# State-major order of the sread tokens, batch 1's sums later, and a rearranged start of batch 0, in an attention and feed-forward kernel

## The chip, the cores and the metric

The kernel runs on one core of a Trainium2 chip. The metric is device time in microseconds (us) of one execution, lower is better.

Engine names: TensorE (PE in the profile, PEld for its weight loads), VectorE (DVE), ScalarE (ACT), GpSimd (POOL), SyncE (SP; SPq is its queue of DMA issues). PSUM is the memory into which the matmuls here write. The "granted clock" is the share of TensorE's full rate that the profile's clock records show; time for which there is no record counts as 1.00.

## The reference

Eight batches of eight heads. `x` holds 512 tokens of 64 values per head, `state` 32. Each attends to the other, and all 544 rows of a batch then go through one feed-forward layer.

```python
scores = scale * x @ state.T ;  a  = softmax(scores)  ; xread = a  @ state   # 512 rows a batch
scores2 = scale * state @ x.T;  a2 = softmax(scores2) ; sread = a2 @ x       # 32 rows a batch
rows = concatenate([xread, sread], axis=2)         # 544 rows a batch, 8 batches
h = rows @ w_in ;  out = (h * sigmoid(h)) @ w_out  # 4352 x 512, float32
```

## The kernel before

For batch `b`, "G1" is the first product of the feed-forward layer (with `w_in` folded into the state as `W1`), "G2" the second. `aT` holds the normalised attention weights of a batch, transposed (the other operand of G1), `stT` the transposed state, and `es` sums of the exponentials over tokens, by which sread is divided. The 32 sread rows of all 8 batches are gathered in `xmT` and done at the very end as 256 tokens, in two tiles of 128 (`tt` 0 and 1). Row `544*b + 512 + n` of the output is state `n` of batch `b`. The parts that matter:

```python
xmT = pers.tile([128, 2, 4, 128], BF16)          # token = 32 * (b % 4) + n
out_sread = out.rearrange("(bb s) m -> bb s m", s=544)
...
# start of batch 0
nc.scalar.activation(warm[:], warm[:], func=EXP, bias=0.0)        # loads the exp table (1.28 us)
nc.sync.dma_start(st0_f[:], state[0].rearrange("h n d -> n h d"))
for hg in range(2):                                               # then x, 512 KB each
    nc.sync.dma_start(x_f[:, ds(4 * hg, 4), :, :], ...)
...
cast_x(0, nc.vector, h0=0, nh=4)
pe_transpose_x(0, 0, 2, ...)       # TensorE; VectorE and ScalarE copy the halves out of PSUM
cast_x(0, nc.vector, h0=4, nh=4)
...
scores(0, 0); exps(0, 0)
pe_transpose_x(0, 1, 2, ...)
scores(0, 1); exps(0, 1)
...
def token_sums(b):                 # VectorE: es, sums of exp over the 4 tokens of a partition
    ...
def sread(b):                      # TensorE: ones x es, then x_nat x exp_nat, into ps
    ...
    nc.vector.reciprocal(rb[:], ps[:, 1, :, :, :])
    for g in range(2):
        for u in range(2):
            nc.vector.tensor_tensor(
                xmT[rows, b // 4, k2, ds(32 * (b % 4), 32)],
                ps[rows, 0, k2, u ^ g, :], rb[rows, k2, u ^ g, :], op=MULT)
...
# between batch 0 and batch 1
for ft in range(NFT):
    ...
    if ft == 4:
        token_sums(1)
    if ft == 13:
        sread(1)
    ...
    G2(0, 3, ft)
...
# steady state: batch b runs, batch n = b + 1 is prepared
    if at == (1, 0):  norm(n, hg), ...          # at = (tile, step)
    if at == (1, 8):  token_sums(n)
    if at == (2, 8):  w1_chunks(n, (0, 1), both) # VectorE and ScalarE copy W1 out of PSUM
    if at == (3, 10): sread(n)
...
# the end: store of tile 0, then tile 1 in two halves of 256 columns
nc.sync.dma_start(out_sread[ds(4 * tt, 4), ds(512, 32), :], o[:])
nc.sync.dma_start(out_sread[ds(4 * tt, 4), ds(512, 32), cols], o[:])
```

In the traces VectorE starts its instructions in the order of the program: after the change, the token sums of batch 2 (62.09 us) stand before the copies of W1 (64.92 us), as in the code.

The softmax here doesn't subtract the row's maximum and nothing guards it: scores larger than these inputs give would overflow.

## Time and profile before

| | before |
|---|---|
| time, median of the first 3 runs | 229.88 us (229.19 to 230.03) |
| span of the profiled run | 228.3 us |
| TensorE busy | 213.5 us (94%) |
| first G1 of batch 0 | 13.26 us |
| first G1 of batch 1 | 46.35 us |
| first G1 of batch 2 | 65.59 us |
| start of the last matmul | 220.94 us |
| last DMA issue; it has landed | 221.71; 227.36 us |

From the page: busy time and share of each engine, then the chain of work that ended last, by engine.

```profile
span 228.3 us, 3733 instructions
...
PE 213.5 (94%) x1462; PEld 102.4 (45%) x1488; DVE 103.2 (45%) x186; ACT 142.5 (62%) x241; POOL 45.8 (20%) x64
...
PE 88%; DVE 6%; issue 1%; ACT 1%; POOL 0%; POOLq 0%
```

By stage (the view of windows; columns: the stretch, its length, busy us and instructions of TensorE, its weight loads, VectorE, ScalarE, GpSimd, then TensorE's granted clock, the share of DMA engines that were busy, GB/s):

```profile
0.00:14.56 14.56, 11.38 (x66) 5.40 (x68) 8.17 (x22) 5.90 (x10) 9.41 (x18) 1.00 1.01 189
...
57.00:197.00 140.00, 138.42 (x948) 63.76 (x963) 68.03 (x115) 100.26 (x163) 28.42 (x36) 1.00 0.40 106
...
213.00:229.00 16.00, 8.22 (x55) 5.10 (x53) 1.54 (x3) 0.98 (x2) 0.00 (x0) 0.90 0.16 49
```

From 57 to 197 us TensorE is busy 138.4 of 140 us: nothing but less TensorE work helps there. The last row is different: 8.2 us of TensorE work in the 15.35 us that are left of the span. The same view by microseconds at the end:

```profile
220.00:221.00 1.00, 1.00 (x12) 0.84 (x9) 0.00 (x0) 0.00 (x0) 0.00 (x0) 1.00 0.28 14
221.00:222.00 1.00, 0.22 (x2) 0.00 (x0) 0.42 (x1) 0.00 (x0) 0.00 (x0) 1.00 0.20 49
...
223.00:224.00 1.00, 0.00 (x0) 0.00 (x0) 0.00 (x0) 0.00 (x0) 0.00 (x0) 1.00 0.27 101
224.00:225.00 1.00, 0.00 (x0) 0.00 (x0) 0.00 (x0) 0.00 (x0) 0.00 (x0) 1.00 0.27 95
225.00:226.00 1.00, 0.00 (x0) 0.00 (x0) 0.00 (x0) 0.00 (x0) 0.00 (x0) 0.84 0.27 96
226.00:227.00 1.00, 0.00 (x0) 0.00 (x0) 0.00 (x0) 0.00 (x0) 0.00 (x0) 0.50 0.19 66
```

TensorE's work ends at 221.2 us and VectorE's last copy at 221.7 us. After that the core waits more than 5 us for its own stores, while its 16 DMA engines show a mean share of only 0.27.

TensorE's waits (who waited for whom, us in total, times, longest):

```profile
PE ps_sr L307 <- DVE es L299: 1.2, 1, 1.2
PE ps_st L217 <- DVE st_b L124: 0.8, 1, 0.8
...
PE ps_sr L307 <- DVE es L300: 0.5, 1, 0.5
```

And what VectorE and TensorE do around those two waits for `es` (start, length, engine, line, operation; in brackets the idle time just before it and what ended it):

```profile
42.40 1.98 DVE L296 TENSOR_REDUCE es_f<-exp_nat 128x128 f32<-128x512 bf16 x2
...
44.81 0.71 DVE L300 TENSOR_TENSOR es<-es_f,es 128x256 bf16<-128x256 f32 x1
...
44.83 0.28 PE L307 MATMUL ps_sr<-es,ones 128*128 128x256 bf16 x1 [1.21 <-DVE es L299]
...
45.44 0.41 DVE L124 COPY aT<-ps_at 128x512 bf16<-128x512 bf16 x1
...
46.35 0.59 PE L376 MATMUL h_664<-aT,W_400 128*128 128x512 bf16 x2
```

Batch 1's first G1 (46.35 us) needs `aT`, which VectorE copies only at 45.44 us, after the token sums.

### The profile page before, as it was taken

What the parts mean: (1) busy time and instruction counts of PE and PEld (TensorE: products, weight loads), DVE (VectorE), ACT (ScalarE), POOL (GpSimd) and SP (SyncE); (2) the same over time, 40 slices, a digit from 0 to 9 for tenths busy, and PEclk for the clock granted to TensorE, in tenths of its full rate; (3) what the DMA queues carried; (4) which work ended last, traced back from release to release, by engine and by line L of the source; (5) the groups of instructions that cost most, each with busy time, mean ns of one, the idle gap of its engine ahead of it and who ended that gap; (6) DMA issues with size and microseconds to landing.
All of it is one profiled execution on the core that took longest, in us unless ns stands there. A gap on an engine that the chain in (4) does not pass through costs nothing.

```text
span 228.3 us, 3733 instructions
## 1 busy us (share of the span) xinstructions
PE 213.5 (94%) x1462; PEld 102.4 (45%) x1488; DVE 103.2 (45%) x186; ACT 142.5 (62%) x241; POOL 45.8 (20%) x64
## 2 busy tenths in 40 slices
PE   7799899799999999999999999999999999999970
PEld 2534335344435443544354534444444444566550
DVE  5554946960765075516552565247434634100110
ACT  2555558679865985598558856885679477444110
POOL 8380001710450045003600260025001200000000
PEclk9999999999999999999999999999999999999997
DMA  6999974585169115911591159113611311111111
GB/s 191 184 196 196 204 226 140 184 199 126 51 128 275 56 48 130 284 46 50 112 296 51 49 121 283 61 46 92 141 47 46 95 46 46 46 49 41 51 24 68
DMA packets 33933, 26.97 MB, mean 118 GB/s; under 512 B 22012, under 2 KB 27900, under 8 KB 33916
## 3 DMA queue, kind: packets, MB, share of 16 engines
q1 hardware_dynamic: 27244, 15.21, 25.6%
q0 software_dynamic: 6672, 11.54, 22.6%
q8 instruction: 11, 0.18, 0.3%
q14 instruction: 6, 0.05, 0.1%
HBM read 17.30 MB, written 8.91 MB: 115 GB/s over the span
## 4 chain that ended last, share of the span: by engine, by line
PE 88%; DVE 6%; issue 1%; ACT 1%; POOL 0%; POOLq 0%
PE o L405 46%; PE ps_sc L244 2%; PE ps_sr L317 2%; PE o_half L427 2%; PE ps_xt L185 1%; PE ps_busy L130 1%; PE o_a L405 1%; DVE rs L266 1%; DVE es_f L296 1%; PE ps_sr L307 1%; DVE rb L326 1%; DVE W_214 L124 1%; ACT exp_nat L256 1%; ACT xT_143 L122 1%; DVE x_nat_141 L101 0%
## 5 line engine op out<-in xcount | busy, mean ns | idle before, releaser
L405 PE MATMUL o<-w_out_sb,g 128*128 128x512 bf16 x489 | 132.1, 380 | 0.5
L405 PEld LDWEIGHTS <-g 128*128 128x128 bf16 x528 | 50.0, 98 | 58.6 <-issue 7.1
L124 DVE COPY o_sb<-o 128x512 f32<-128x512 f32 x17 | 11.8, 692 | 64.4 <-PE o L405 64.1
L269 POOL TENSOR_TENSOR an<-exp_nat,rc 128x512 bf16<-128x512 bf16 (+1 forms) x16 | 15.9, 1009 | 111.2 <-DVE rc L267 111.0
L326 DVE RECIPROCAL rb<-ps_sr 128x256 f32<-128x256 f32 x8 | 14.1, 1758 | 16.6 <-PE ps_sr L317 16.6
L122 ACT ACTIVATE o_sb<-o 128x512 f32<-128x512 f32 x15 | 8.9, 596 | 13.5 <-PE o L405 5.3
L296 DVE TENSOR_REDUCE es_f<-exp_nat 128x128 f32<-128x512 bf16 x16 | 15.3, 1000 | 0.0
L266 DVE TENSOR_REDUCE rs<-exp_nat 128x16 f32<-128x512 bf16 x16 | 10.6, 660 | 2.2 <-ACT exp_nat L256 1.5
L96 POOL DMA_DIRECT2D x_f<-in_x_dram x7 | 6.5, 924 | 20.6 <-DVE x_nat_486 L101 19.1
L256 ACT ACTIVATE exp_nat<-ps_sc 128x512 bf16<-128x512 f32 x16 | 8.8, 595 | 1.1 <-PE ps_sc L244 1.0
L386 PEld LDWEIGHTS <-w_in_sb 128*128 128x128 bf16 x64 | 6.3, 98 | 3.9
L256 ACT ACT_TABLE_LOAD x6 | 7.7, 1283 | 0.1
L553 ACT ACT_TABLE_LOAD x6 | 7.7, 1283 | 0.1
L330 DVE TENSOR_TENSOR xmT<-ps_sr,rb 64x64 bf16<-64x64 f32 x32 | 7.1, 222 | 0.6
L350 PEld LDWEIGHTS <-stT 64*32 64x32 bf16 x264 | 2.8, 89 | 9.1 <-issue 8.5
L130 PE MATMUL ps_busy<-busy 128*128 128x512 bf16 x11 | 5.4, 627 | 1.4 <-DVE busy L144 1.2
L405 PE MATMUL o_a<-w_out_sb,g 128*128 128x512 bf16 x15 | 5.8, 396 | 0.1
L376 PEld LDWEIGHTS <-W_214 128*128 128x128 bf16 x32 | 3.2, 106 | 5.1 <-DVE W_214 L124 1.5
L300 DVE TENSOR_TENSOR es<-es_f,es 128x256 bf16<-128x256 f32 x8 | 5.1, 638 | 0.3
L376 PEld LDWEIGHTS <-W_400 128*128 128x128 bf16 x32 | 3.1, 98 | 3.9 <-issue 0.3
L307 PE MATMUL ps_sr<-es,ones 128*128 128x256 bf16 x16 | 3.2, 273 | 1.7 <-DVE es L299 1.2
L376 PEld LDWEIGHTS <-W_1420 128*128 128x128 bf16 x32 | 3.1, 98 | 3.6 <-issue 0.2
(518 smaller groups left out, 351.1 us busy)
## 6 DMA issues: line engine op xcount, KB each, us to landing
out_dram<-o_sb SPq DMA_DIRECT2D x33, 256.0 KB, 2.4
x_f<-in_x_dram POOLq DMA_DIRECT2D x7, 1024.0 KB, 7.0
w_in_sb<-in_moe_w_in_dram POOLq DMA_DIRECT2D x3, 512.0 KB, 11.5
w_out_sb<-in_moe_w_out_dram POOLq DMA_DIRECT2D x3, 512.0 KB, 14.1
x_f<-in_x_dram SPq DMA_DIRECT2D x2, 512.0 KB, 4.4
st_f<-in_state_dram SPq DMA_DIRECT2D x8, 64.0 KB, 11.3
w_in_sb<-in_moe_w_in_dram POOLq DMA_DIRECT2D x2, 256.0 KB, 7.6
w_out_sb<-in_moe_w_out_dram POOLq DMA_DIRECT2D x2, 256.0 KB, 8.2
```

What stands on the lines that cost most here:

```text
L122: nc.scalar.activation(dst, src, func=COPY, bias=0.0)
L124: eng.tensor_copy(dst, src)
L130: nc.tensor.matmul(ps[:], busy[:, 0:128], busy[:], start=True, stop=True, skip_group_check=True)
L256: nc.scalar.activation(e[:], sc_ps[hg][:], func=EXP, bias=0.0, scale=SCALE)
L266: nc.vector.tensor_reduce(rs[:], e[:], axis=AX, op=ADD)
L269: eng.tensor_tensor(a[:, ds(c, n)], e[:, ds(c, n)], rc[:, ds(c, n)].to_broadcast([128, n, 4, NS]), op=MULT,)
L296: nc.vector.tensor_reduce(f[:, hg], exp_nat[b, hg].rearrange("p c s n -> p s n c"), axis=AX, op=ADD)
L326: nc.vector.reciprocal(rb[:], ps[:, 1, :, :, :])
L330: nc.vector.tensor_tensor(xmT[rows, b // 4, k2, ds(32 * (b % 4), 32)], ps[rows, 0, k2, u ^ g, :], rb[rows, k2, u ^ g, :], op=MULT,)
L376: nc.tensor.matmul(ps[:], W1[b][:, hg, ds(128 * ft, 128)], aT[b][:, hg, :, :], start=(hg == 0), stop=(hg == 1), skip_group_check=True,)
L405: nc.tensor.matmul(outs[tt][:], gt[b * NFT + ft][:, ds(128 * tt, 128)], w_out_sb[:, ft, :], start=(ft == 0), stop=(ft == NFT - 1), skip_gr ...
L553: nc.scalar.activation(warm[:], warm[:], func=SILU, bias=0.0)
```

## The change

Four things at once. (1) The tokens of the sread tiles go in state-major order, `4 * n + b`, so that the outermost dimension of the stores in memory is 32 states and no longer 4 batches. (2) Batch 1's token sums and sread leave the gap between batches 0 and 1. (3) State 0 is loaded from ScalarE's queue, so that SyncE can issue `x` sooner. (4) Each cast of `x` in batch 0 is split over VectorE and ScalarE, and all its transposes come before the first scores.

```diff
-    xmT = pers.tile([128, 2, 4, 128], BF16)
+    xmT = pers.tile([128, 2, 4, NS, 4], BF16)
-    out_sread = out.rearrange("(bb s) m -> bb s m", s=544)
+    out_sread = out.rearrange("(bb s) m -> s bb m", s=544)
...
+    nc.scalar.dma_start(st0_f[:], state[0].rearrange("h n d -> n h d"))
     nc.scalar.activation(warm[:], warm[:], func=EXP, bias=0.0)
-    nc.sync.dma_start(st0_f[:], state[0].rearrange("h n d -> n h d"))
...
-    cast_x(0, nc.vector, h0=0, nh=4)
-    pe_transpose_x(0, 0, 2, ...)
-    cast_x(0, nc.vector, h0=4, nh=4)
+    for hg, pool, tag in ((0, psO, "o"), (1, psH, "h1")):
+        cast_x(0, nc.vector, 0, 2, 4 * hg, 4)
+        cast_x(0, nc.scalar, 2, 2, 4 * hg, 4)
+        pe_transpose_x(0, hg, 2, ...)
...
-                    xmT[rows, b // 4, k2, ds(32 * (b % 4), 32)],
+                    xmT[rows, b // 4, k2, :, b % 4],
...
-                    xmT[:, :, kt, :],
+                    xmT[:, :, kt].rearrange("p t n b -> p t (n b)"),
...
-            nc.sync.dma_start(out_sread[ds(4 * tt, 4), ds(512, 32), :], o[:])
+            nc.sync.dma_start(out_sread[ds(512, 32), ds(4 * tt, 4), :], o[:])
...                                                  # the half stores likewise
-    pe_transpose_x(0, 1, 2, ...)                    # from between the scores of batch 0
...
-        if ft == 4:
-            token_sums(1)
-        if ft == 13:
-            sread(1)
...
                     upto(NFT * b + min(lead + ft, NFT))
+                    if b == 1 and ft == 2:
+                        token_sums(1)
+                if b == 1 and at == (1, 4):
+                    sread(1)
```

More of the change, by code (lines that the diff above doesn't have):

```diff
@@ L100, in cast_x @@
             x_nat[b] = xpool.tile([128, 4, H, D], BF16, tag="x_nat", name=f"x_nat{b}")
-        eng.tensor_copy(
+        copy(
+            eng,
             x_nat[b][:, ds(c0, nc_), ds(h0, nh), :],
@@ L190, in pe_transpose_x @@
             copy(engs[u], xT[b][:, ds(m * u, m), ds(2 * hg, 2), :], ps[:])
-    cast_x(0, nc.vector, h0=0, nh=4)
-    pe_transpose_x(0, 0, 2, lambda sh, dt, nm: psO.tile(sh, dt, tag="o", name=nm))
-    cast_x(0, nc.vector, h0=4, nh=4)
+    for hg, pool, tag in ((0, psO, "o"), (1, psH, "h1")):
+        cast_x(0, nc.vector, 0, 2, 4 * hg, 4)
+        cast_x(0, nc.scalar, 2, 2, 4 * hg, 4)
+        pe_transpose_x(0, hg, 2, lambda sh, dt, nm: pool.tile(sh, dt, tag=tag, name=nm))
     nc.vector.memset(st_f[:, :, 0:1, 0:1], 0.0)
@@ L436, in last_half @@
         copy(nc.vector, o[:], ps[:, 0 : DM // 2])
-        nc.sync.dma_start(out_sread[ds(4 * tt, 4), ds(512, 32), cols], o[:])
+        nc.sync.dma_start(out_sread[ds(512, 32), ds(4 * tt, 4), cols], o[:])
     both = (nc.vector, nc.scalar)
@@ L449 @@
     exps(0, 0)
-    pe_transpose_x(0, 1, 2, lambda sh, dt, nm: psH.tile(sh, dt, tag="h1", name=nm))
     scores(0, 1)
```

## The prediction

> **What bounds it now.** TensorE: in the page it is busy 94% of a 228.3 us span and holds 88% of the chain that ended last; from 57 to 197 us (windows view) it is busy 138.4 of 140 us. The change touches three stretches outside that.
>
> 1. Tail. The last copy ends near 221.7 us, the span at 228.3. One-microsecond windows show a DMA share of 0.20 to 0.28 from 220 to 226 us, some 96 GB/s: 512 KB drains through about 4 of 16 engines. A normal 256 KB store lands 2.05 us after issue; the last 128 KB here 5.7 us after (221.71 to 227.4). The store's outer dimension in memory is 4 batches. [...]
>
> 2. Between batch 0 and 1. The waits view: TensorE waits 1.2 us for es (cast) and 0.5 us for es (subtract), 43.6 to 45.6 us; VectorE's token sums also delay the copy of aT (45.44 us).
>
> 3. Head. First G1 matmuls at 13.3 to 14 us, behind cast, transpose, scores, exp, norm.
>
> **What the change does.**
>
> Tail: with 32 states outermost, 16 engines share each store; the last should land 1.95 us after issue instead of 5.7. Saved: 3.7 us, all on the chain. The token order inside xmT should cost nothing: the matmul still reads one contiguous row.
>
> Middle: token sums (3.0 us of VectorE) leave the gap; aT is copied at about 43.5 us, so batch 1's first G1 comes at about 44.05 instead of 46.35 us. The sread matmuls (0.68 us) return later: net 1.6 us. But VectorE gets 2.7 us (reciprocal 1.76, four multiplies 0.93) between batch 2's norm and its token sums, ahead of its W1 copies. Before, VectorE is busy almost unbroken from 59.2 to 65.7 us, and batch 2's first G1 starts at 65.59, soon after the W1 copy of 64.39 to 65.07. That copy now ends near 67.6 (old times), TensorE wants it at 66.3: a new stall of about 1.3 us. Net gain of the middle: 0.3 us (0 to 1.4).
>
> Head: x is issued 0.47 us sooner, but VectorE can't cast before its stT copies end at 5.01 us. Half casts take 0.53 and 0.34 us on VectorE, about 0.6 on ScalarE (by its 512-column copies). ScalarE then carries cast, copy, cast, copy, exp, exp: the first exp ends near 9.8 us (8.93 before), the second near 10.4 (10.87). VectorE's sums and GpSimd's multiplies then run back to back and end near 12.9 us (12.80). Gain: 0 (−0.5 to +0.4).
>
> Sum: 229.88 − 3.7 − 0.3 − 0 = 225.9; I put it at 225.8 us, 1.8% under: the middle can gain more than lose. Range 224.9 to 226.7; chances 0.30 faster by over 2%, 0.69 within, 0.01 slower.
>
> **What would show it.** Tail: DMA share near 1 in short bursts, span end 3 us after the last copy. Middle: no wait of TensorE for es near 44 us; a new wait of 1.3 us for VectorE's copy of W1 at batch 2's first G1. Head: exp of group 0 later, of group 1 earlier, first G1 within 0.5 us of 13.3.
>
> **What would make it wrong.** VectorE reaching the W1 copy sooner (no stall: 224.5); stores scattered over 4 batches writing slower than in row order; ScalarE's chain in the head shorter or longer than counted.

The tail's term stands on numbers of the trace of the kernel before. The three sread stores, with 4 batches outermost, show a share of 0.27 of the 16 engines from 223 to 226 us (0.27 × 16 = 4.3), and each one's semaphore is raised by one early landing and then 4. The normal 256 KB store before them (128 rows of 2 KB, issued at 215.03 us) landed 2.05 us after issue, and its semaphore was raised 16 times. That 16 engines would share a store with 32 states outermost was the expectation, which no trace had shown yet; the 1.95 us for the last 128 KB is an estimate, a little under the 2.05 us of twice the size. Measured were 16 landings and 2.06 us, and a share of 0.94 in a burst ("The result", experiments 1, 5 and 6).

## The result, and the profile after

The changed kernel took 226.03 us in the median of 4 runs (225.01 to 226.66); the kernel before, in the same rounds and earlier, 229.64 us (229.19 to 230.03). The ratio is 0.9837 (95% interval 0.9801 to 0.9874), clear of noise, as the interval excludes 1. A ratio here and below is the mean time of one kernel's runs over that of the other's of the same rounds, so it is not quite the ratio of the medians that are quoted. The forecast was 225.8 us.

The profiled runs, stretch by stretch (each from one trace, differences worked out from the starts). In both, TensorE reaches full rate late, at 17.4 to 17.5 us, so that they may be compared; "The clock" below shows that this was not sure to happen.

| stretch | before | after | difference |
|---|---|---|---|
| start to first G1 of batch 0 | 13.26 | 13.46 | +0.20 |
| to first G1 of batch 1 | 33.09 | 30.91 | −2.18 |
| to first G1 of batch 2 | 19.24 | 21.30 | +2.06 |
| to start of the last matmul | 155.35 | 155.37 | +0.02 |
| to the end of the span | 7.41 | 3.81 | −3.60 |
| span | 228.35 | 224.85 | −3.50 |

So up to the last matmul the changed kernel has gained nothing (220.94 against 221.04 us); the whole gain comes after it. The end, in the same view as above:

```profile
220.00:221.00 1.00, 1.00 (x11) 0.89 (x10) 0.03 (x1) 0.00 (x0) 0.00 (x0) 1.00 0.50 186
221.00:222.00 1.00, 0.31 (x3) 0.03 (x1) 0.42 (x1) 0.00 (x0) 0.00 (x0) 1.00 0.39 131
222.00:223.00 1.00, 0.00 (x0) 0.00 (x0) 0.00 (x0) 0.00 (x0) 0.00 (x0) 1.00 0.00 1
223.00:224.00 1.00, 0.00 (x0) 0.00 (x0) 0.00 (x0) 0.00 (x0) 0.00 (x0) 1.00 0.38 130
224.00:225.00 1.00, 0.00 (x0) 0.00 (x0) 0.00 (x0) 0.00 (x0) 0.00 (x0) 1.00 0.00 0
```

Now each store is a short burst (from about 219.6, 221.2 and 223.0 us on), and the engines are idle between them, so that a window of 1 us shows the mean of both. The repeat of the changed kernel (experiment 4) has a half microsecond that a burst fills, at a share of 0.94 and 356 GB/s:

```profile
219.50:220.00 0.50, 0.50 (x7) 0.45 (x5) 0.25 (x1) 0.00 (x0) 0.00 (x0) 1.00 0.94 356
```

SyncE issues the last store at 221.80 us and it has landed at 223.86 us, 2.06 us later; before the change it was 5.65 us.

TensorE's waits after the change: both waits for `es` are gone, a wait for W1 is new, and the wait for the cast of the state (`st_b`, in batch 0) is longer, 1.1 us against 0.8. The third line is new too: state 0 now lands later (experiment 9).

```profile
PE h L378 <- DVE W L125: 1.1, 1, 1.1
PE ps_st L219 <- DVE st_b L125: 1.1, 1, 1.1
...
PE ps_st L163 <- DVE st_n L125: 0.5, 1, 0.5
```

The gap between the batches, and then the new wait. `aT` is copied at 43.81 us, G1 starts at 44.37 us; but at 64 us VectorE still has the token sums of batch 2 to do, and TensorE stands idle for 1.10 us until it has copied W1:

```profile
43.81 0.42 DVE L125 COPY aT<-ps_at 128x512 bf16<-128x512 bf16 x1 [0.96 <-PE ps_at L288]
...
44.37 0.81 PE L378 MATMUL h<-aT,W 128*128 128x512 bf16 x3
```

```profile
59.09 1.69 DVE L328 RECIPROCAL rb<-ps_sr 128x256 f32<-128x256 f32 x1
...
60.82 1.24 DVE L332 TENSOR_TENSOR xmT<-ps_sr,rb 64x64 bf16<-64x64 f32 x4
...
62.09 2.01 DVE L298 TENSOR_REDUCE es_f<-exp_nat 128x128 f32<-128x512 bf16 x2
...
64.47 0.43 DVE L302 TENSOR_TENSOR es<-es_f,es 128x256 bf16<-128x256 f32 x1
64.92 1.29 DVE L125 CAST W<-ps_w 128x512 bf16<-128x512 f32 x2
...
65.67 0.61 PE L378 MATMUL h<-aT,W 128*128 128x512 bf16 x2 [1.10 <-DVE W L125]
```

The first two of these lines, the reciprocal and the four multiplies of batch 1's sread, are what was put in front. The multiplies that write `xmT` have become slower (minimum, median, maximum in ns), before and then after:

```profile
L330 DVE TENSOR_TENSOR xmT<-ps_sr,rb x32: 216/222/228, 24.2 to 189.9; 64x64 bf16<-64x64 f32 x32
```

```profile
L332 DVE TENSOR_TENSOR xmT<-ps_sr,rb x32: 291/300/310, 24.3 to 190.2; 64x64 bf16<-64x64 f32 x32
```

### The profile page after: what moved, and what is told of

It is laid out like the page before. It is cut to its first block, busy times and chain, and to the rows that moved or that the text cites. A ratio compares the mean times of both kernels' runs of the same rounds, so it can differ in the third digit from the quotient of the medians. Undisturbed runs are those within 1.5% of the kernel's fastest.

```text
span 224.8 us, 3735 instructions
## 1 busy us (share of the span) xinstructions
PE 214.2 (95%) x1462; PEld 102.1 (45%) x1488; DVE 104.4 (46%) x186; ACT 143.5 (64%) x243; POOL 45.4 (20%) x64
## 4 chain that ended last, share of the span: by engine, by line
PE 86%; DVE 6%; ACT 3%; DMA 1%; issue 1%; POOL 0%; DVEq 0%; ACTq 0%
PE o L407 45%; PE h L378 25%; PE ps_w L352 4%; PE h L388 3%; PE o_half L429 2%; PE ps_sc L246 2%; DVE rb L328 2%; PE ps_sr L319 1%; DMA st_f<-in_state_dram 1%; PE o_a L407 1%; PE ps_xt L186 1%; DVE xmT L332 1%; DVE W L125 1%; DVE es_f L298 1%; ACT exp_nat L258 1%
## 5 line engine op out<-in xcount | busy, mean ns | idle before, releaser
L399 ACT ACTIVATE g<-h 128x512 bf16<-128x512 f32 (+1 forms) x144 | 82.2, 573 | 45.0 <-PE h L378 30.7
L378 PE MATMUL h<-aT,W 128*128 128x512 bf16 x256 | 76.5, 383 | 1.7 <-DVE W L125 1.1
L125 DVE COPY o_sb<-o 128x512 f32<-128x512 f32 x17 | 11.8, 692 | 62.7 <-PE o L407 62.5
L378 PEld LDWEIGHTS <-W 128*128 128x128 bf16 x256 | 25.0, 99 | 32.1 <-DVE W L125 3.1
L125 DVE CAST W<-ps_w 128x512 bf16<-128x512 f32 (+1 forms) x31 | 20.0, 676 | 18.5 <-PE ps_w L352 18.5
L123 ACT ACTIVATE W<-ps_w 128x512 bf16<-128x512 f32 (+1 forms) x35 | 18.7, 575 | 9.4 <-PE ps_w L352 9.3
L125 POOL CAST x_nat<-x_f 128x512 bf16<-128x512 f32 x24 | 14.7, 646 | 0.0
L352 PE MATMUL ps_w<-w_in_sb,stT 64*32 64x512 bf16 (+1 forms) x264 | 11.5, 383 | 0.0
L332 DVE TENSOR_TENSOR xmT<-ps_sr,rb 64x64 bf16<-64x64 f32 x32 | 9.6, 300 | 0.6
L388 PE MATMUL h<-xmT,w_in_sb 128*128 128x256 bf16 x64 | 9.6, 273 | 0.0
## 6 DMA issues: line engine op xcount, KB each, us to landing
w_out_sb<-in_moe_w_out_dram POOLq DMA_DIRECT2D x3, 512.0 KB, 13.3
```

What stands on the lines that cost most here:

```text
L123: nc.scalar.activation(dst, src, func=COPY, bias=0.0)
L125: eng.tensor_copy(dst, src)
L332: nc.vector.tensor_tensor(xmT[rows, b // 4, k2, :, b % 4], ps[rows, 0, k2, u ^ g, :], rb[rows, k2, u ^ g, :], op=MULT,)
L352: nc.tensor.matmul(pss[f, hg][ds(32 * s, 32), 0:n], stT[ds(r, 64), b, h // 2, s % 2, :], w_in_sb[ds(r, 64), h // 2, ds(f, n)], start=True, ...
L378: nc.tensor.matmul(ps[:], W1[b][:, hg, ds(128 * ft, 128)], aT[b][:, hg, :, :], start=(hg == 0), stop=(hg == 1), skip_group_check=True,)
L388: nc.tensor.matmul(ps[:, 0:256], w_in_sb[:, kt, ds(128 * ft, 128)], xmT[:, :, kt].rearrange("p t n b -> p t (n b)"), start=(kt == 0), stop ...
```

## The experiments

Each edit is against the kernel named. Times are medians with their range; the kernel before was timed in the same rounds on the same chip (its medians were 229.2 to 229.9 us).

### 1. The stores alone: `tail`

The kernel before with part (1) of the change and nothing else.

```diff
-    out_sread = out.rearrange("(bb s) m -> bb s m", s=544)
+    out_sread = out.rearrange("(bb s) m -> s bb m", s=544)
...      # with it xmT's tile, its write and read, and the three stores, as in the change
```

> The kernel before with the state-major order alone (token order of xmT and the three stores of the sread rows). Theory (the gain is all in the last stores, because they use 16 engines instead of 4): 3.5 us less than the kernel before, ratio 0.984 to 0.986, span end about 2.5 us after the last copy instead of 6.6; the xmT writes 0.30 us each instead of 0.22. Rival (the middle and the head carry some of the gain): less than 2.5 us saved.

Measured: 226.08 us (225.65 to 227.32, 6 runs) against 229.19, ratio 0.9855 (0.9812 to 0.9899). From the start of the last matmul to the end of the span 3.80 us, against 7.41 in the kernel before. This one part is as fast as the whole change, whose repeat on the same chip is at 0.9858 (experiment 4). The span ends 3.06 us after the last copy, where 2.5 were expected. The theory stands: the gain is in the stores.

### 2. The middle alone: `mid`

The kernel before with part (2) alone.

```diff
-        if ft == 4:
-            token_sums(1)
-        if ft == 13:
-            sread(1)
...      # batch 1: token_sums(1) at tile 0, step 2; sread(1) at tile 1, step 4
```

> The kernel before with batch 1's token sums and sread moved later, alone. Theory (2.3 us won at batch 1's first G1, given back as 0.68 us of sread matmuls and a new wait of TensorE for VectorE's copy of W1 at batch 2's first G1): within 0.6 us of the kernel before, the first G1 of batch 1 at 44.05 us instead of 46.35, the new wait 1.1 to 1.4 us. Rival (the gap was worth 1.6 us and the stall seen in the changed kernel comes of its other parts): 1.3 us or more saved.

Measured: 229.68 us (228.44 to 230.55, 6 runs) against 229.19, ratio 0.9997 (0.9952 to 1.0043). First G1 of batch 1 at 44.03 us. The new wait for W1 is there, 0.9 us (1.1 to 1.4 were expected), with 0.4 us more for `aT`; from the first G1 of batch 1 to that of batch 2 it is 21.15 us instead of 19.24. In the traces the 1.9 us are given back in full; the timed runs alone would leave room for a gain or loss of 1 us.

### 3. The head alone: `head`

The kernel before with parts (3) and (4).

```diff
-    nc.sync.dma_start(st0_f[:], ...)             # and on ScalarE's queue instead
-    cast_x(0, nc.vector, h0=0, nh=4)             # and the loop over both halves instead
-    pe_transpose_x(0, 1, 2, ...)                 # from between the scores
```

> The kernel before with the head alone: state of batch 0 on ScalarE's queue, casts on two engines, transposes in one row. Theory: no gain, 0 to 0.4 us slower: the state lands near 3.7 us instead of 2.76, so VectorE's stT copies end 0.5 us later and its first cast with them, and ScalarE's chain does the rest. Rival (the head won something and other parts hid it): 0.3 us or more faster.

Measured: 229.89 us (228.79 to 231.09, 6 runs) against 229.19, ratio 1.0009 (0.9959 to 1.0059). No gain. First G1 of batch 0 at 13.46 us. The interval is too wide to tell 0 from a loss of 0.4 us; the traces say more, below. ScalarE's chain in batch 0, first in the kernel before and then with the new head (these lines are from the trace of the changed kernel, whose head is the same; `head` itself shows them at most 0.07 us later): there are two more copies of 0.6 us in it (the casts, at 5.02 and 7.63 us), so that the first exp starts 1.1 us later and both end at 10.63 us, where the second ended at 10.87.

```profile
8.33 0.60 ACT L256 ACTIVATE exp_nat<-ps_sc 128x512 bf16<-128x512 f32 x1 [0.48 <-PE ps_sc L244]
...
10.27 0.60 ACT L256 ACTIVATE exp_nat<-ps_sc 128x512 bf16<-128x512 f32 x1 [0.49 <-PE ps_sc L244]
```

```profile
5.02 0.63 ACT L123 ACTIVATE x_nat<-x_f 128x512 bf16<-128x512 f32 x1 [2.31 <-DMA x_f<-in_x_dram]
...
7.63 0.62 ACT L123 ACTIVATE x_nat<-x_f 128x512 bf16<-128x512 f32 x1
...
8.95 0.60 ACT L123 ACTIVATE xT<-ps_xt 128x512 bf16<-128x512 bf16 x1 [0.70 <-PE ps_xt L186]
9.44 1.19 ACT L258 ACTIVATE exp_nat<-ps_sc 128x512 bf16<-128x512 f32 x2
```

### 4. The changed kernel again: `again`

No edit.

> The changed kernel once more, because its four runs fell into two pairs (225.0 and 225.4; 226.6 twice). If the spread is noise of the runs, 225.0 to 226.7 again with a mean near 225.9; if one pair was a rare state, nearly all runs in one of them.

Measured: 226.48 us (225.34 to 227.27, 6 runs), ratio 0.9858 (0.9815 to 0.9901). The spread is that of the first four runs, a little wider (to 227.27), and every kernel that was timed several times shows one of 0.7 us or more; where it comes from is asked under "the clock" below.

### 5 and 6. Batch-major order, other cuts of the store: `store_2b` and `store_1b`

The kernel before, token order as it was, each store cut by batches: `m = 2` gives two DMAs of two batches, `m = 1` four of one batch.

```diff
-        nc.sync.dma_start(out_sread[ds(4 * tt, 4), ds(512, 32), cols], o[:])
+        for i in range(0, 4, m):
+            nc.sync.dma_start(
+                out_sread[ds(4 * tt + i, m), ds(512, 32), cols], o[ds(32 * i, 32 * m), :])
```

> The kernel before, batch-major order kept, each sread store cut into two of 2 batches. Theory [...]: 2 engines instead of 4, about 24 GB/s each, so 512 KB drain in 10 to 11 us instead of 5.4: about 5 us slower, DMA share near 0.13 in the tail. Rival (the 4-batch stores were slow because of their row addresses or their extra issue time): no such doubling.

> The kernel before, batch-major order kept, each sread store cut into four of 1 batch. Theory: outermost size is then 32, so all 16 engines: 2.0 to 3.6 us faster than before; what is missing to 3.6 us is the issue of three more stores (0.33 us each at least, and the last one lands about 2 us after its own issue). VectorE's xmT writes stay at 0.22 us. Rival (state-major addresses themselves are what writes fast): at most 1 us faster.

Measured: `store_2b` 234.92 us (one look), 5.6 us more than the 229.32 of the kernel before; `store_1b` 227.21 us (226.65 to 227.84, 4 runs), ratio 0.9896 (0.9862 to 0.9929), 2.1 us less. The end of `store_2b` in two-microsecond windows (the columns as above):

```profile
220.00:222.00 2.00, 0.16 (x2) 0.00 (x0) 0.42 (x1) 0.00 (x0) 0.00 (x0) 1.00 0.13 44
...
224.00:226.00 2.00, 0.00 (x0) 0.00 (x0) 0.00 (x0) 0.00 (x0) 0.00 (x0) 0.50 0.13 38
...
228.00:230.00 2.00, 0.00 (x0) 0.00 (x0) 0.00 (x0) 0.00 (x0) 0.00 (x0) 0.50 0.14 48
```

The share is halved, 0.13 to 0.14 where it was 0.27, and so is the rate: 38 to 50 GB/s where it was some 96. Of the core's 16 engines these shares make about 2 (0.13 × 16 = 2.1) and about 4 (0.27 × 16 = 4.3), with 2 and 4 batches outermost in memory; the bursts of the state-major stores, with 32 states outermost, make 15 (0.94 × 16, in `again`). The rates agree: a packet of 2 KB took 84 ns in the tail of the kernel before (the median from 221 us on), which is 24.4 GB/s, so that 2 at a time make 49 GB/s and 4 make 98. The packed traces show the same order in another count: leaving out one early update in the first two, the semaphore of the very last store is raised by 4 landings in the kernel before (226.55 to 227.36 us), by 2 in `store_2b` (230.79 and 231.66 us), and by 16 in `store_1b` and in the changed kernel (223.68 to 223.86 us there). The same bytes to the same addresses from the same partitions are slower with two batches in a DMA than with four, and faster with one, an order that no account by row addresses gives. What other sizes than these would do, no run here shows; so the general rule that the expectation of `store_2b` gave is cut. `store_1b` wins less than the state-major store because SyncE issues its DMAs one after the other: the last is issued at 223.54 us instead of 221.80, and lands at 225.09 us. From the start of its last matmul (221.05 us) to the end of the span it is 4.95 us, against 7.41 in the kernel before and 3.81 in the changed one.

### 7. The stall taken out: `later`

The changed kernel, with batch 2's token sums moved behind its first W1 copies on VectorE.

```diff
-                    if at == (1, 8):
+                    if at == ((2, 10) if b == 1 else (1, 8)):
                         token_sums(n)
```

> The changed kernel with batch 2's token sums moved from tile 1, step 8 to tile 2, step 10, behind its first W1 copies on VectorE. Theory (VectorE's queue makes TensorE wait for W1): the wait of 0.9 to 1.1 us at batch 2's first G1 is gone, first G1 of batch 2 about 20.2 us after that of batch 1 instead of 21.3; 0.9 to 1.1 us faster than the changed kernel, ratio to the kernel before 0.980 to 0.982. Rival (another wait lies right behind it: aT's transpose, a PSUM bank): less than 0.4 us gained.

Measured: 225.12 us (224.64 to 225.72, 6 runs) against 229.32, ratio 0.9805 (0.9777 to 0.9833). TensorE has no wait for W1 left; first G1 of batch 2 comes 20.06 us after that of batch 1, instead of 21.30. VectorE copies W1 first (62.60 us), TensorE's G1 follows at 64.77 us without a wait, while VectorE is still at its sums:

```profile
62.60 1.29 DVE L125 CAST W<-ps_w 128x512 bf16<-128x512 f32 x2 [0.18 <-PE ps_w L352]
...
63.92 1.98 DVE L298 TENSOR_REDUCE es_f<-exp_nat 128x128 f32<-128x512 bf16 x2
...
64.77 0.59 PE L378 MATMUL h<-aT,W 128*128 128x512 bf16 x2
...
66.26 0.43 DVE L302 TENSOR_TENSOR es<-es_f,es 128x256 bf16<-128x256 f32 x1
```

So the gain of the middle was real, and of the 2.06 us that were given back 1.24 were due to VectorE's queue order. The other 0.82, the 0.68 us of sread matmuls among them, stay. This is read from the traces: the ratios point the same way, but their intervals overlap (0.9777 to 0.9833 here, 0.9815 to 0.9901 for `again`).

### 8. Which side of `xmT` pays for the order: `contig`

The changed kernel, with `xmT` written as before and read with steps by the matmul.

```diff
-    xmT = pers.tile([128, 2, 4, NS, 4], BF16)
+    xmT = pers.tile([128, 2, 4, 4, NS], BF16)
-                    xmT[rows, b // 4, k2, :, b % 4],
+                    xmT[rows, b // 4, k2, b % 4, :],
-                    xmT[:, :, kt].rearrange("p t n b -> p t (n b)"),
+                    xmT[:, :, kt].rearrange("p t b n -> p t n b"),
```

> The changed kernel with xmT written in batch order (contiguous) and read in state order by the matmul (32 elements apart). Theory (the 0.30 us of the writes comes of their 8-byte steps): writes back at 0.22 us, and the first wait for the state cast 0.8 us again instead of 1.1. Open: whether TensorE reads the strided columns as fast; if it does, its 64 matmuls stay at 273 ns and the last stage at its length; if not, they are longer.

Measured: 245.84 us (one look). The writes are back at 222 ns and the wait for the state's cast at 0.8 us, as expected, but the 64 matmuls that read `xmT` take more than twice as long:

```profile
L388 PE MATMUL h<-xmT,w_in_sb x64: 587/607/608, 196.0 to 231.9; 128*128 128x256 bf16 x64
```

In the changed kernel the same line has a median of 273 ns. The last matmul starts at 240.25 us instead of 221.04, 19 us later. Reading bfloat16 at steps of 64 bytes is what costs (607 ns against 273); writing it at steps of 8 bytes costs 0.08 us an instruction (300 ns against 222, or 35%). Why either is slower, no run here shows.

### 9. The head without the moved state load: `casts`

The kernel before with part (4) alone; the state is still issued first, by SyncE.

```diff
-    cast_x(0, nc.vector, h0=0, nh=4)             # and the loop over both halves instead
-    pe_transpose_x(0, 1, 2, ...)                 # from between the scores
     nc.sync.dma_start(st0_f[:], ...)             # stays
```

> The kernel before with casts on two engines and transposes in one row, but the state load still first on SyncE's queue. Theory (in the head, moving the state load is what costs, as it then travels beside x and lands at 3.72 us instead of 2.76): the state lands near 2.8 us again, VectorE's stT copies end near 5.0 us and its first half cast starts there instead of at 5.58; first G1 0.3 to 0.5 us sooner than with the whole head in the same clock state (13.46 us when TensorE is at half rate until 17 us), total within 1 us of the kernel before. Rival (ScalarE's chain of cast, copy, cast, copy sets the pace whatever the state does): first G1 at 13.3 to 13.5 us in that clock state.

Measured: 229.52 us (229.23 to 229.93, 4 runs) against 229.89, ratio 0.999 (0.9955 to 1.0025). The state landed at 2.59 us and VectorE's `stT` copies ended at 5.01 us, as the theory has it. But in this run `x` landed only at 5.56 us, so the casts began at 5.58 us all the same, and the first G1 was at 13.46 us to the hundredth as in the whole head. The forecast of 0.3 to 0.5 us fell. What can be said is that the chain from the casts on sets the 13.46 us; the price of the state load by itself stays open.

What the state load does can still be read from all traces. With the old order of issue (eight traces) the state landed at 2.59 to 2.76 us and the first half of `x` at 4.68 to 4.98 us in six of them, at 5.02 and 5.56 in two. With the state on ScalarE's queue (all six traces) the state landed at 3.72 to 4.23 us and `x` at 4.99 to 5.52 us, though its issue is 0.47 us sooner. Issuing them side by side made the state later and `x` no sooner.

### 10. The fast middle and stores with the old head: `later_oldhead`

Parts (1) and (2) and the edit of experiment 7, on the kernel before:

```diff
-                    if at == (1, 8):
+                    if at == ((2, 10) if b == 1 else (1, 8)):
                         token_sums(n)           # parts (3) and (4) left out
```

> The kernel before with the state-major stores, batch 1's sums later and batch 2's token sums behind its W1 copies, but the old head. Theory (the new head is worth nothing, the stores 3.5 us, the middle without its stall 1.3 us): as fast as the same with the new head (225.1 us there), within 0.4 us; ratio to the kernel before near 0.980. Rival (the new head helps once the stall is gone): over 0.5 us slower than that.

Measured: 224.60 us (224.42 to 225.13, 5 runs) against 229.89, ratio 0.9776 (0.9742 to 0.9811), the lowest ratio, with the change's head left out. The intervals of this run and of `later` (0.9805) overlap. Those of this run and of `tail` (0.9855, 0.9812 to 0.9899), which has the stores alone, do not, if only just: the mended middle is worth something in the timed runs too.

### 11 and 12. More warm-up matmuls: `fill` and `oldhead_fill`

`fill` is `later` with three more full-size warm-up matmuls in the head; `oldhead_fill` is `later_oldhead` with one. "Warm-up" is only the name here for the matmuls of `keep_busy`, whose result is not used; whether more of them bring the clock up sooner is what was to be tested.

```diff
# fill
-    keep_busy(6, psH, "h1")
+    keep_busy(7, psH, "h1")
-    keep_busy(3, psH, "h1")
+    keep_busy(4, psH, "h1")
         pe_transpose_x(0, hg, 2, ...)
+        if hg == 0:
+            keep_busy(1, psA, "a3")
# oldhead_fill
-    keep_busy(3, psH, "h1")
+    keep_busy(4, psH, "h1")
```

> The changed kernel with batch 2's token sums later and three more warm-up matmuls in the head (one before the state's transposes, one after, one between the two rows of transposes of x). Theory (the 1 to 2 us of spread of every kernel comes of TensorE's clock in the head: at half rate until 17 us in some runs, at full rate from 4.5 us in others): [...]mean 0.3 to 0.9 us below the 225.1 us without them, first G1 near 12 us. Rival (the fillers only take TensorE's time, the clock does what it did): same mean within 0.3 us or slower, spread as before.

> The fastest form so far (old head, state-major stores, batch 1's sums later, batch 2's token sums behind its W1 copies) with one more warm-up matmul, in the 0.6 us in which TensorE otherwise waits for the first cast of x (5.58 to 6.17 us). Theory [...]: 224.0 to 224.6 us, highest run under 225.0. Rival (one matmul does not change the lottery of the clock): 224.4 to 225.2 as without it, ratio near 0.978.

Measured: `fill` 224.48 us (224.32 to 225.24, 5 runs), ratio 0.9779 (0.9747 to 0.9811), on the same chip and rounds as `later_oldhead` and equal to it. Its median is 0.64 us under that of `later` (225.12), as forecast, but that was another chip, and the intervals of the two ratios overlap. First G1 of its profiled run at 13.31 us, not near 12, though its clock was full from 7.12 us. `oldhead_fill` 224.24 us (223.87 to 226.16, 6 runs), ratio 0.9799 (0.9765 to 0.9832): five runs at or under 224.74, one at 226.16, where the forecast had none above 225.0. Both are inconclusive: they are among the fastest kernels, and neither shows that the added matmuls are the reason.

### The clock

Why does every kernel spread by 0.7 us and more? In the profiled runs TensorE starts at half rate (a warm-up matmul of 512 columns every 0.43 us) and reaches full rate (0.22 us) at very different times. Two traces of kernels whose heads are the same, first that of the kernel before, then that of `store_1b`; each shows three warm-up matmuls and then four matmuls of batch 0's first two G1:

```profile
4.12 1.46 PE L130 MATMUL ps_busy<-busy 128*128 128x512 bf16 x3
...
13.26 1.31 PE L376 MATMUL h_248<-aT,W_214 128*128 128x512 bf16 x2
...
14.36 1.06 PE L376 MATMUL h_253<-aT,W_214 128*128 128x512 bf16 x2
```

```profile
4.10 0.82 PE L130 MATMUL ps_busy<-busy 128*128 128x512 bf16 x3
...
11.81 0.38 PE L376 MATMUL h<-aT,W 128*128 128x512 bf16 x1
...
12.49 0.81 PE L376 MATMUL h<-aT,W 128*128 128x512 bf16 x3 [0.30 <-DVE aT L124]
```

In the kernel before the rate doubles near 17 us; in `store_1b` at 4.0 us; in `tail` and `mid` it doubles at 4.2 to 4.3 us, falls back at 7.6 to 7.7 us and stays down for 10.24 us (the exact times here and in the table are those of the clock records in the packed traces). In `store_1b`, `tail` and `mid` the rise comes 2.75 to 3.05 us after the first matmul (1.23 us). The clock records of five traces show drops to half rate, of 3.41, 6.83 (`later`) or 10.24 us (`tail`, `mid`). What sets the time of the rise and the length of the drops is not shown. The page alone can mislead here: it gives a granted clock of 1.00 over the first 14.56 us of the kernel before, whose matmuls run at half rate there, because the clock records of that trace start only at 17.47 us; the spacing of the matmuls is what to trust.

The record has one more sign that the clock makes the spread. Each timed run has a mean granted clock. Of the ten runs of the changed kernel (`after` and `again`), the five at 1.000 took 226.36 to 226.66 us, the three at 0.999 took 225.01 to 225.44 (the other two, at 0.992 and 0.985, took 225.80 and 227.27); in `later` the three at 1.000 took 225.11 to 225.12 us, the two at 0.984 took 225.71 and 225.72. In `oldhead_fill`, though, three runs at 0.992 took 224.09, 224.39 and 226.16. How often each case occurs, and that it makes up the whole spread, no run here shows.

First G1 of batch 0, sorted by it:

| clock in the head | old head | new head |
|---|---|---|
| half rate past the first G1 (full from 16.6 to 17.5 us) | 13.26 (before) | 13.46 (after, `head`, `casts`), 13.45 (`again`) |
| half rate until 11.68 us | none | 13.88 (`contig`) |
| full early, dropped at 7.6 to 7.7 us | 12.84 (`tail`), 12.85 (`mid`) | none |
| full from 7.1 us or sooner, up to 11.8 us at least | 11.81 (`store_1b`), 12.00 (`later_oldhead`), 12.14 (`store_2b`), 12.17 (`oldhead_fill`) | 12.84 (`later`), 13.31 (`fill`) |

At half rate the new head is 0.2 us slower (`contig` is not comparable: its clock rose before the first G1, and `x` landed late, at 5.52 us). At full rate there are two traces of it, `fill`, which has more matmuls in its head than any other, and `later`, whose clock fell back at 11.88 us. `later` is some 0.7 us or more behind: GpSimd's last multiply, ahead of that first G1, ends at 12.38 us, against 11.52 (`store_1b`) and 11.71 us (`later_oldhead`). A faster TensorE shortens only its own share of the chain, and the new head has put two casts of 0.62 us onto ScalarE's share. That this is the whole reason was only argued.

## Why the prediction was right, point by point

- **Total.** 225.8 us was forecast, 226.03 measured (226.48 in the repeat). Right, and within 2% as the likeliest case. That it fits to 0.2 us is partly luck: the four runs fall into two pairs (225.01 and 225.44, 226.62 and 226.66), and the median lies between them. In the two traces the difference is 3.50 us, where the parts of the forecast add up to 4.0.
- **Tail.** Forecast 3.7 us, measured 3.60 us in the traces; the last store lands 2.06 us after issue (1.95 forecast), the span ends 3.1 us after the last copy (3). Experiments 1, 5 and 6 show that the number of engines is the cause (2, 4 and 16 landings at 48, 96 and, in a burst, 356 GB/s). A part of the old tail was a slow start: from 220 to 221 us the DMA engines were as busy as later (a share of 0.28) but moved 14 GB/s; in the same microsecond `mid` shows 18 GB/s at 0.30, `head` and `casts` 8 GB/s at 0.18. Why is open; the traces with state-major stores have no such microsecond.
- **Middle.** Forecast: first G1 of batch 1 2.3 us sooner, 0.68 us of sread matmuls back, a new stall of 1.3 us. Measured: 2.18 us less from G1 to G1 in the first stretch, 2.06 us more in the second, of which 1.10 us are the stall and 0.68 the matmuls; 0.28 us are not accounted for. Experiment 2 gives the net 0 by itself (in its trace; its timed runs do so within 1 us), and experiment 7 removes the stall and keeps the gain.
- **Head.** Forecast 0, and first G1 within 0.5 us of 13.3: it came at 13.46. The reasoning had two errors. It expected the cast to begin at 5.01 us, when `stT` was done; but the state, now beside `x`, landed 1 us later, and the copies ended at 5.55. And it took the clock of the one trace it had for the clock of all runs; at full rate the new head seems to lose more.
- **The step that was wrong:** "The token order inside xmT should cost nothing". The read by the matmul costs nothing (273 ns before and after), but the write does: 300 ns instead of 222, 1.24 instead of 0.93 us for a batch, which TensorE sees twice. In batch 0 it waits 0.3 us more for the state's cast that stands behind them (`tail` 1.1 us, `contig` 0.8). And batch 1's multiplies stand in front of batch 2's W1 copy: from batch 1's first G1 to batch 2's it is 20.98 us in `contig`, which writes in the old order, against 21.30 in the changed kernel. So they took a part of the middle's gain as well. It is the small term of a sum of 3.6 us.

## What to carry to other kernels

Look at the outermost dimension in memory of the last stores of a kernel: nothing hides them, and here a share of 0.27 of the DMA engines, while nothing else ran, went with 4 batches outermost, and bursts of 0.94 with 32 states. When work is moved off a critical gap, follow the queue of the engine that does it to the place where it lands: here it landed in front of a copy that TensorE needs, and moving one more item behind that copy won back 1.24 us in the traces. If a layout must have steps on one side, put them on the write that is done once (here 0.08 us more for each of 32) and not on the operand that TensorE streams 64 times (0.33 us more each).
